# Chunk attention and two block products: another layout of the attention's score tiles, and part of one weight matrix split in place

## The chip, the cores and the metric

One Trainium2 chip, one of its cores. The metric is the device time of one execution of the kernel in microseconds, the median of several runs. The engines of the core are TensorE (PE; its weight loads are listed as PEld), VectorE (DVE), ScalarE (ACT), GpSimd (POOL) and SyncE (SP), which issues the DMA transfers.

## The reference

```python
def _attn_ref(q, k, v):                      # 8 x 8 heads x 576 x 64
    ...
    scores = scale * np.matmul(q_c, k_c.transpose(0, 1, 2, 4, 3))   # chunks of 64
    scores = scores - np.max(scores, axis=-1, keepdims=True)
    attn = np.exp(scores)
    attn = attn / (np.sum(attn, axis=-1, keepdims=True) + 1e-09)
    out = np.matmul(attn, v_c)
    ...
def reference(...):
    x = attention's output as 4608 tokens x 512
    x = square(relu(x @ moe_w_in)) @ moe_w_out        # 512 -> 2048 -> 512
    h = x @ moe2_w_in                                 # 512 -> 2048
    g = where(h >= 1, h, where(h <= -1, 0, (h + 1) ** 2 / 4))
    return g @ moe2_w_out                             # 2048 -> 512
```

All four weight matrices reach the kernel as 64-bit floats and are decoded to 32 bits on chip.

## The kernel before, in words

All large products are made in `float32r`: an operand is split into a rounded part (hi) and the rest (lo), and three products hi*hi, lo*hi, hi*lo go into one PSUM tile.

The work runs in four stages on TensorE. **Stage 1** (attention and the first matrix): the plain product `plain_h` (line 402) makes one 128x512 block `ph` of `x @ w_in` out of 12 matmuls of 512 columns, in two slots of six; there are 9 blocks of 512 tokens with 16 rows of `ph` each, so 288 slots. **Stages 2 to 4** are the three other products, done as block products with seven products P1 to P7 in place of eight (`form_b`, `form_a`, line 449 `products`).

The order of all instructions is written out by hand, with a slot number for every step: in a slot first TensorE's six matmuls are put down, then what `at_slot` has for it. Each engine does its instructions in that order.

*Attention.* A unit is four heads (two pairs `p` of two heads `e`) of two chunks `c` of 64 tokens; there are 72 units. The first 11 turns come ahead of stage 1 (`head`); after that a turn has four slots (`turn`): slot 0 has `att_d` of unit i-3, `att_b` of unit i-1 and `att_x` of unit i-3; slot 1 `att_exp` of i-1; slot 2 `att_c`, `att_ce` of i-2 and `att_n` of i-1; slot 3 `att_a`, `att_ae` of unit i. On TensorE a unit is:

- `att_a`, tile `psA` (line 291): four 128x128 transposes of q and k;
- `att_b`, tile `psB` (line 309): eight matmuls of 64x64 with 64 columns in f32, the scores. The contraction lies on the partitions of head `e`; the result goes to the partitions of chunk `c`. In the order of the loops the quadrants of the array (rows `e`, columns `c`) are (0,0), (0,1), (1,0), (1,1), and the same again for the second pair;
- `att_c`, tile `psC` (line 350): eight matmuls of 64x64 with the identity, which transpose the weights `s` of one chunk and head each; quadrants (0,0), (1,1), (0,0), (1,1) and so on;
- `att_d`, tile `psD` (line 367): eight matmuls of 64x64, the weights times v.

*Weights.* `w_out` of the first expert (m = 0) and the two matrices of the second (m = 1, 2) go through 16 units each, one every 5.1 slots from slot 22 on: `unit_a` and `unit_b` decode and round, `sums` makes three more blocks of the seven, `unit_c` casts all seven blocks (128x896) to hi on ScalarE, `unit_hi` stores hi to a DRAM tile (448 KB), `unit_d` subtracts on VectorE and stores lo (448 KB). `load_w` (line 243) later reads one product's hi and lo for both columns, 256 KB in one transfer, into one of the 56 tiles `w0` to `w55`. For m = 0 the first 24 loads (products P1, P5, P6; eight row blocks each) stand at every second slot from slot 192 on; their tiles are `w32` to `w55`, which nothing used before.

Of the kernel before, what the change touches and what calls it, by code (L numbers as in the profile page):

```python
# [8 lines left out]
F32 = mybir.dt.float32  # L9
F32R = mybir.dt.float32r  # L10
U32 = mybir.dt.uint32
AF = mybir.ActivationFunctionType
ALU = mybir.AluOpType
AX = mybir.AxisListType

P = 128

TINY = 2.0**-15 * 1.125
CH = 64
G = 32  # L20
HU = 4
NP = HU // 2
# [1 line left out]

FMAX = 3.4028234663852886e38
RANK = ("P1", "P5", "P6", "P3", "P7", "P2", "P4")
CIDX = {"P1": 0, "P2": 1, "P7": 2, "P4": 3, "P5": 4, "P6": 5, "P3": 6}
SIZES = (448, 448, 448, 480, 480)


# [1 line left out]
def chunk_attention_moe_moe2(ctx, tc, q, k, v, w_in1, w_out1, w_in2, w_out2, out):  # L32
# [10 lines left out]
    nc = tc.nc  # L43
# [4 lines left out]
    NF = DFF // P  # L48
# [4 lines left out]
    HF = NF // 2  # L53
# [5 lines left out]
    NBL = len(blocks)  # L59
# [3 lines left out]
    wp = ctx.enter_context(tc.tile_pool(name="wp", bufs=1))  # L63
# [6 lines left out]
    def f(ap):  # L70
        return ap.bitcast(F32)
# [26 lines left out]
    wd = {(m, a): dram.tile([P, 2, 2, 7, P], F32, name=f"w{m}_{a}") for m in range(3) for a in range(8)}  # L98
# [4 lines left out]


    win = {}
    wst = {}

    def bits(t, a, y):
# [71 lines left out]

    def sums(c):

        for o, x, z, op in ((4, 2, 3, ALU.add), (2, 0, 2, ALU.subtract), (5, 4, 0, ALU.subtract), (6, 1, 5, ALU.subtract)):
            nc.gpsimd.tensor_tensor(out=c[:, o], in0=c[:, x], in1=c[:, z], op=op)

    def store_parts(m, a, b, hi, lo):
        nc.sync.dma_start(out=wd[m, a][:, 0, b], in_=f(hi))
        nc.sync.dma_start(out=wd[m, a][:, 1, b], in_=f(lo))

    def unit_b(m, a, b):  # L190
        y, ab = wst[m, a, b]
        if m == 2:
            c = ep.tile([P, 4, P], F32, tag="wl", name="wq", bufs=2, padded_shape=[P, 7, P])
        else:
            c = ep.tile([P, 7, P], F32, tag="wc", name="wc", bufs=1)
        nc.vector.scalar_tensor_tensor(
            out=c[:, 0:4].rearrange("p a f -> p (a f)"), in0=ab, scalar=TINY, in1=f(y), op0=ALU.is_ge, op1=ALU.mult
        )
        wst[m, a, b] = c
        if m == 2:  # L200
            nc.sync.dma_start(out=wq[a, b], in_=c[:, 0:4])
            del wst[m, a, b]
        else:
            sums(c)

    def unit_c(*u):
        c = wst[u]
        hi = ep.tile([P, 7, P], F32R, tag="wh", name="wh", bufs=2)
        nc.scalar.copy(hi, c)
        wst[u] = (c, hi)  # L210

    def unit_hi(m, a, b):
        nc.sync.dma_start(out=wd[m, a][:, 0, b], in_=f(wst[m, a, b][1]))

    def unit_d(m, a, b):
        c, hi = wst.pop((m, a, b))
        lo = ep.tile([P, 7, P], F32R, tag="wl", name="wl", bufs=2)
        nc.vector.tensor_tensor(out=lo, in0=c, in1=f(hi), op=ALU.subtract)
        nc.sync.dma_start(out=wd[m, a][:, 1, b], in_=f(lo))


    def late_a(a, b):
# [4 lines left out]
    def late_b(a, b):  # L227
        sums(wst[a, b])
# [7 lines left out]
    def late_d(a, b):  # L236
        c, hi = wst.pop((a, b))
        nc.gpsimd.tensor_tensor(out=c, in0=c, in1=f(hi), op=ALU.subtract)
        store_parts(2, a, b, hi, c)

    wt = {}

    def load_w(m, tag, a, prod):
        t = wp.tile([P, 2, 2, P], F32R, tag=f"w{tag}", name=f"w{m}")
        nc.sync.dma_start(out=f(t), in_=wd[m, a][:, :, :, CIDX[prod]])
        wt[m, a, prod] = t
# [5 lines left out]
    def rows(par):  # L252
        return slice(par * CH, (par + 1) * CH)
# [48 lines left out]
    def att_b(u):  # L302

        qkT = att[u]
        pt = pa.tile([P, 2, 512], F32, tag="qk", name="psB")
        for p in range(NP):
            for e in range(2):
                for c in range(2):
                    nc.tensor.matmul(  # L309
                        pt[rows(c), e, p * CH:(p + 1) * CH],  # L310
                        qkT[rows(e), 0, p, rows(c)],
                        qkT[rows(e), 1, p, rows(c)],
                        start=True,
                        stop=True,
                    )
        sc = pt[:, :, 0:NP * CH].rearrange("q e (p k) -> q e p k", p=NP)
        m = ep.tile([P, 2, NP], F32, tag="m", name="m", bufs=3)
        z = ep.tile([P, NP, 2], F32, tag="z", name="z", bufs=3)
        nc.vector.tensor_reduce(out=m, in_=sc, op=ALU.max, axis=AX.X, negate=True)  # L319
        att[u] = [sc, m, z]  # L320

    def att_exp(u):
        sc, m, z = att[u]
        s = ep.tile([P, NP, 2, CH], F32, tag="s", name="s", bufs=2)
        for p in range(NP):
            for e in range(2):
                nc.scalar.activation(
                    out=s[:, p, e],
                    in_=sc[:, e, p],
                    func=AF.Exp,  # L330
                    bias=m[:, e, p:p + 1],
                    accum_out=z[:, p, e:e + 1],
                )
        att[u] = [s, z]

    def att_n(u):
        s, z = att[u]
        nc.vector.tensor_scalar_add(z, z, 1e-9)
        nc.vector.reciprocal(z, z)
        s4 = s.rearrange("q p e k -> q (p e) k")  # L340
        z4 = z.rearrange("q p e -> q (p e)")
        nc.gpsimd.tensor_tensor(out=s4, in0=s4, in1=z4.unsqueeze(2).to_broadcast([P, HU, CH]), op=ALU.mult)

    def att_c(u):
        s, _ = att[u]
        pt = pa.tile([P, NP, 2, CH], F32, tag="t", name="psC", padded_shape=[P, HU, 2, CH], bufs=2)
        for p in range(NP):
            for e in range(2):
                for c in range(2):
                    nc.tensor.matmul(  # L350
                        pt[rows(c), p, e, :], s[rows(c), p, e, :], ident[rows(c), rows(c)], start=True, stop=True
                    )
        att[u] = pt

    def att_ce(u):
        at = ep.tile([P, NP, 2, CH], F32, tag="atT", name="atT", bufs=2)
        nc.scalar.copy(at, att[u])
        att[u] = at

    def att_d(u):  # L360

        at = att[u]
        pt = pa.tile([P, 2, 512], F32, tag="d", name="psD")
        for p in range(NP):
            for c in range(2):
                for e in range(2):
                    nc.tensor.matmul(  # L367
                        pt[rows(e), c, p * CH:(p + 1) * CH],
                        vt[u // UT % NV][rows(c), u % UT * HU + 2 * p + e, :],
                        at[rows(c), p, e, :],  # L370
                        start=True,
                        stop=True,
                    )
        att[u] = pt
# [250 lines left out]
    SB1 = 2 * NF * NBL  # L625
# [19 lines left out]
    def at_slot(s, fn, *args):  # L645
        s = int(s)
        assert cur[0] is None or s >= cur[0], (s, cur)
        todo.setdefault(s, []).append((fn, args))
# [4 lines left out]
    with tc.manual_schedule():  # L653
        early = tc.tile_pool(name="early", bufs=1, side="right")
        ep = early.__enter__()
        ident = ep.tile([P, P], F32, name="ident")
        plain = tc.tile_pool(name="plain", bufs=1, space=bass.MemoryType.PSUM)
        pa = plain.__enter__()
# [89 lines left out]
        for n, u in enumerate(units):  # L748
            g = U0 + n * UPER
            if n < 2:  # L750
                at_slot(g - 3 + n, stage_unit, *u)
            at_slot(g, unit_a, *u)
            if n + 2 < len(units):
                at_slot(g, stage_unit, *units[n + 2])
            at_slot(g + 2, unit_b, *u)
            if u[0] < 2:
                at_slot(g + 4, unit_c, *u)
                at_slot(g + 5, unit_hi, *u)
                at_slot(g + 6, unit_d, *u)
# [26 lines left out]
        for w, s0 in ((0, SB1), (1, SB2)):  # L786
            for j in range(NPAIR):
                for r, prod in enumerate(RANK):
                    s = s0 + 56 * j + 8 * r
                    for kk in range(HF):  # L790
                        pe_slot(s + kk, form_b, w, j, prod, kk)
                    for kp in range(HF // 2):
                        t = s + 2 * kp - PREP
                        if j == 0 and r == 0 and w == 0:
                            t = max(t, done + 12)
# [13 lines left out]
        for j in range(NPAIR):  # L809
            for i in range(HF):  # L810
                b = SA2 + 7 * (HF * j + i)
                for prod, o in OFFS.items():
                    pe_slot(b + o, form_a, j, i, prod)
        for j in range(NPAIR):
            if j == 0:
                e = SA2
                loads = tuple(e - 24 + n for n in range(4))
                times = dict(P1=e - 14, P5=e - 11, P6=e - 8, P3=e - 6, P2=e - 3, P7=e - 2, P4=e + 1)
            else:
                b = SA2 + 7 * (HF * j - 1)  # L820
# [9 lines left out]
            if j + 1 < NPAIR:  # L830
                for n in range(4):
                    g = SA2 + 56 * j + 12 + 10 * n
                    u = divmod(4 * j + n, 2)
# [4 lines left out]
        for t in range(56):  # L838
            r, kk = divmod(t, 8)
            i, ro = divmod(t, 7)  # L840

            tag = (t + 2 * NF) % 56
            s = 2 * NF * (NBL - 3) + 2 * t if t < 24 else 2 * NF * (NBL - 1) + 2 * (t - 24) + 1 if t < 32 else SB1 + t - 30
            at_slot(s, load_w, 0, tag, kk, RANK[r])
            at_slot(SB1 + 56 * (NPAIR - 1) + t, load_w, 1, tag, i, ORD[ro])
            at_slot(SA2 + 7 * (HF * (NPAIR - 1) + i) + OFFS[ORD[ro]], load_w, 2, tag, kk, RANK[r])

# [54 lines left out]
```

## Time and profile before

| what | value |
|---|---|
| median of 3 runs | 1654.92 us (1653.35 to 1658.9) |
| the profiled execution, its own time | 1659.15 us |
| span of its trace, first to last instruction | 1657.4 us |
| TensorE busy | 1617.0 us (98%) |
| VectorE, ScalarE, GpSimd busy | 1077.6, 873.8, 422.4 us |
| DMA moved | 339.6 MB, mean 205 GB/s |

The table is read from the top of the profile: the span is what a sum of terms is made against, and the 1.75 us between span and time lie around it. An engine's busy share is a mean over four stages that differ.

### The profile page before, as it was taken

How to read it: one execution, taken by the hardware profiler on the slowest of the kernel's cores; microseconds unless marked ns; L12 is line 12 of the kernel's file. 1: busy time of each engine (PE TensorE's matmuls, PEld its weight loads, DVE VectorE, ACT ScalarE, POOL GpSimd, SP SyncE). 2: the span in 40 equal slices, each digit the busy share in tenths (PEclk: the TensorE clock that was granted, in tenths of full speed). 3: DMA queues.
4: the chain of work that ended last, by engine and by line, in shares of the span. 5: the costliest groups of instructions: out<-in, count | busy, mean ns of one | idle time of the engine just before them, and what ended most of it. 6: DMA issues, size and time to landing. Idle time of an engine off the chain costs nothing.

```text
span 1657.4 us, 29362 instructions
## 1 busy us (share of the span) xinstructions
PE 1617.0 (98%) x10512; PEld 1376.6 (83%) x10512; DVE 1077.6 (65%) x1432; ACT 873.8 (53%) x1852; POOL 422.4 (25%) x466
## 2 busy tenths in 40 slices
PE   6999999999999999999999999999999999999998
PEld 4677777777777899999888898988888899998887
DVE  6956555555444177767776757767574777877776
ACT  7656666666554244444444566756565544444442
POOL 2666666565333300000000333424330000000000
PEclk9999999999999999999999999999999999999999
DMA  9768888889996895427277765554659873554723
GB/s 211 204 202 275 275 274 271 267 271 274 268 261 217 279 275 170 132 91 224 64 224 231 214 233 191 197 199 173 226 202 342 292 200 89 146 147 100 198 41 48
DMA packets 442738, 339.60 MB, mean 205 GB/s; under 512 B 214240, under 2 KB 419040, under 8 KB 442592
## 3 DMA queue, kind: packets, MB, share of 16 engines
q1 hardware_dynamic: 442592, 337.73, 67.9%
q8 instruction: 83, 1.36, 0.3%
q14 instruction: 63, 0.52, 0.1%
HBM read 195.04 MB, written 142.61 MB: 204 GB/s over the span
## 4 chain that ended last, share of the span: by engine, by line
PE 85%; DVE 6%; DMA 3%; issue 2%; ACT 2%; POOL 1%; SPq 0%; POOLq 0%; DVEq 0%; ACTq 0%
PE X L453 31%; PE ph L411 24%; PE V L453 16%; PE W L453 7%; PE psC L350 2%; PE psA L291 2%; PE psD L367 1%; PE psB L309 1%; DVE ol L443 1%; DVE wy L118 1%; DMA w<-lc 1%; DVE t L534 1%; DVE wy L115 1%; DVE xr L447 1%; DVE wy L147 1%
## 5 line engine op out<-in xcount | busy, mean ns | idle before, releaser
L453 PE MATMUL X<-oh,w 128*128 128x448 f32 (+1 forms) x1920 | 559.1, 372 | 4.5 <-DVE c L514 4.5
L442 ACT CAST oh<-gr 128x896 fp32r<-128x896 f32 (+1 forms) x280 | 270.0, 964 | 334.9 <-PE X L453 152.1
L443 DVE TENSOR_TENSOR ol<-gr,oh 128x896 fp32r<-128x896 f32 (+1 forms) x280 | 314.3, 1124 | 182.7 <-ACT oh L442 176.9
L453 PEld LDWEIGHTS X<-oh,w 128*128 128x128 f32 x1920 | 360.7, 188 | 48.0 <-ACT t L528 4.3
L453 PE MATMUL X<-ol,w 128*128 128x448 f32 (+1 forms) x960 | 357.0, 372 | 6.8 <-POOL ol L443 5.3
L453 PE MATMUL V<-oh,w 128*128 128x448 f32 (+1 forms) x960 | 278.7, 371 | 0.0
L411 PE MATMUL ph<-xh,ih 128*128 128x512 f32 x576 | 245.9, 427 | 0.0
L411 PE MATMUL ph<-xl,ih 128*128 128x512 f32 x576 | 228.1, 396 | 0.0
L411 PE MATMUL ph<-xh,il 128*128 128x512 f32 x576 | 227.3, 395 | 0.0
L424 POOL TENSOR_TENSOR g<-g 128x512 f32<-128x512 f32 x144 | 169.1, 1174 | 187.1 <-ACT g L423 179.7
L453 PEld LDWEIGHTS X<-ol,w 128*128 128x128 f32 x960 | 180.5, 188 | 29.5 <-POOL ol L443 6.9
L453 PEld LDWEIGHTS V<-oh,w 128*128 128x128 f32 x960 | 180.2, 188 | 21.2 <-ACT s L499 0.3
L447 DVE TENSOR_TENSOR gr<-gr,gr 128x896 f32<-128x896 f32 (+1 forms) x160 | 177.7, 1111 | 2.8 <-DMA gr<-g 2.8
L453 PE MATMUL V<-ol,w 128*128 128x448 f32 (+1 forms) x480 | 177.9, 371 | 0.0
L423 ACT ACTIVATE g<-ph 128x512 f32<-128x512 f32 x144 | 86.3, 600 | 156.1 <-PE ph L411 143.3
L453 PE MATMUL W<-oh,w 128*128 128x448 f32 (+1 forms) x480 | 139.3, 371 | 0.0
L411 PEld LDWEIGHTS ph<-xh,ih 128*128 128x128 f32 x576 | 109.1, 189 | 25.5
L443 POOL TENSOR_TENSOR ol<-xr,oh 128x896 fp32r<-128x896 f32 (+1 forms) x15 | 36.6, 2442 | 364.2 <-ACT oh L442 348.8
L411 PEld LDWEIGHTS ph<-xl,ih 128*128 128x128 f32 x576 | 109.1, 189 | 24.4
L411 PEld LDWEIGHTS ph<-xh,il 128*128 128x128 f32 x576 | 109.7, 190 | 17.4
L528 ACT ACTIVATE t<-c,half 128x448 f32<-128x448 f32 (+1 forms) x120 | 81.2, 681 | 70.4 <-DVE c L514 70.4
L319 DVE TENSOR_REDUCE m<-psB 128x4 f32<-128x256 f32 x72 | 30.4, 422 | 124.6 <-PE psB L309 124.6
(69 smaller groups left out, 1980.1 us busy)
## 6 DMA issues: line engine op xcount, KB each, us to landing
w<-w SPq DMA_DIRECT2D x168, 256.0 KB, 5.0
gr<-g SPq DMA_DIRECT2D x96, 448.0 KB, 5.2
gr<-g SPq DMA_DIRECT2D x64, 480.0 KB, 4.6
g<-t SPq DMA_DIRECT2D x96, 224.0 KB, 2.6
wu<-in_moe_w_out_dram SPq DMA_DIRECT2D x64, 256.0 KB, 4.3
g<-t SPq DMA_DIRECT2D x64, 240.0 KB, 4.6
w<-wh SPq DMA_DIRECT2D x32, 448.0 KB, 3.9
w<-wl SPq DMA_DIRECT2D x32, 448.0 KB, 5.1
```

Source lines behind the costliest of these rows:

```text
L115: nc.vector.scalar_tensor_tensor(out=y, in0=w1, scalar=0xC0000000, in1=y, op0=ALU.bitwise_and, op1=ALU.bitwise_or)
L291: nc.tensor.transpose(pt[:, i, p, :], qkn[i][:, h0 + 2 * p:h0 + 2 * p + 2, :].rearrange("p h d -> p (h d)"), ident)
L319: nc.vector.tensor_reduce(out=m, in_=sc, op=ALU.max, axis=AX.X, negate=True)
L350: nc.tensor.matmul(pt[rows(c), p, e, :], s[rows(c), p, e, :], ident[rows(c), rows(c)], start=True, stop=True)
L411: nc.tensor.matmul(ph, win[fi][wi][:, kt * P:(kt + 1) * P], x[:, i, :], start=(kt == 0 and a == 0), stop=(kt == KT - 1 and a == 2),)
L423: nc.scalar.activation(out=g, in_=ph, func=AF.Relu)
L424: nc.gpsimd.tensor_tensor(out=g, in0=g, in1=g, op=ALU.mult)
L442: nc.scalar.copy(hi, raw)
L443: eng.tensor_tensor(out=lo, in0=raw, in1=f(hi), op=ALU.subtract)
L447: eng.tensor_tensor(out=o, in0=x, in1=z, op=ALU.subtract)
L453: nc.tensor.matmul(o, wt_[:, wi, c, :], x[:, i, :], start=first and a == 0, stop=last and a == 2, skip_group_check=True,)
L528: nc.scalar.activation(out=t, in_=h, func=AF.Square, bias=half, scale=0.5)
```

## The change

In the attention, the scores of a pair `p` of heads go to the partitions `p` and the chunk `c` to the free dimension (before: chunk on the partitions, pair on the free dimension). `att_b` keeps its eight matmuls and its loops, and writes to other quadrants. With this layout `att_c` takes two 128x128 transposes, one for each `e`, for its eight identity matmuls. `att_exp`, `att_n`, `att_ce`, `att_d` and the maximum keep their sizes and index the new order.

In the weights, for m = 0, the hi and lo of P1, P5 and P6 are written by `unit_c` and `unit_d` straight into the tiles `w32` to `w55`, in three casts and three subtracts of 128x128 a unit; the cast, subtract and stores that go by way of DRAM are left with four blocks of seven (128x512, 256 KB each), and the first 24 `load_w` of m = 0 fall away. `CIDX` and `sums` are numbered anew, so that these four blocks lie side by side; the number and size of the sums stay.

```diff
-CIDX = {"P1": 0, "P2": 1, "P7": 2, "P4": 3, "P5": 4, "P6": 5, "P3": 6}
+CIDX = {"P1": 0, "P2": 1, "P7": 2, "P4": 3, "P3": 4, "P5": 5, "P6": 6}
...
+    def w_tag(t):
+        return (t + 2 * NF) % 56
...
-    def unit_c(*u):
-        c = wst[u]
-        hi = ep.tile([P, 7, P], F32R, tag="wh", name="wh", bufs=2)
-        nc.scalar.copy(hi, c)
-        wst[u] = (c, hi)
+    def unit_c(m, a, b):
+        c = wst[m, a, b]
+        if m == 0:
+            for prod in RANK[:3]:
+                if b == 0:
+                    wt[0, a, prod] = wp.tile([P, 2, 2, P], F32R, tag=f"w{w_tag(RANK.index(prod) * HF + a)}", name="w0")
+                nc.scalar.copy(wt[0, a, prod][:, 0, b], c[:, CIDX[prod]])
+        r = unit_r(m)
+        hi = ep.tile([P, r.stop - r.start, P], F32R, tag="wh", name="wh", bufs=2, padded_shape=[P, 7, P])
+        nc.scalar.copy(hi, c[:, r])
+        wst[m, a, b] = (c, hi)
+
+    def unit_r(m):
+        return slice(1, 5) if m == 0 else slice(0, 7)
...
     def unit_d(m, a, b):
         c, hi = wst.pop((m, a, b))
-        lo = ep.tile([P, 7, P], F32R, tag="wl", name="wl", bufs=2)
-        nc.vector.tensor_tensor(out=lo, in0=c, in1=f(hi), op=ALU.subtract)
-        nc.sync.dma_start(out=wd[m, a][:, 1, b], in_=f(lo))
+        r = unit_r(m)
+        if m == 0:
+            for prod in RANK[:3]:
+                t = wt[0, a, prod]
+                nc.vector.tensor_tensor(out=t[:, 1, b], in0=c[:, CIDX[prod]], in1=f(t[:, 0, b]), op=ALU.subtract)
+        lo = ep.tile([P, r.stop - r.start, P], F32R, tag="wl", name="wl", bufs=2, padded_shape=[P, 7, P])
+        nc.vector.tensor_tensor(out=lo, in0=c[:, r], in1=f(hi), op=ALU.subtract)
+        nc.sync.dma_start(out=wd[m, a][:, 1, b, r], in_=f(lo))
...
             for e in range(2):
                 for c in range(2):
                     nc.tensor.matmul(
-                        pt[rows(c), e, p * CH:(p + 1) * CH],
+                        pt[rows(p), e, c * CH:(c + 1) * CH],
                         qkT[rows(e), 0, p, rows(c)],
                         qkT[rows(e), 1, p, rows(c)],
...
-        pt = pa.tile([P, NP, 2, CH], F32, tag="t", name="psC", padded_shape=[P, HU, 2, CH], bufs=2)
-        for p in range(NP):
-            for e in range(2):
-                for c in range(2):
-                    nc.tensor.matmul(
-                        pt[rows(c), p, e, :], s[rows(c), p, e, :], ident[rows(c), rows(c)], start=True, stop=True
-                    )
+        pt = pa.tile([P, 2, NP, CH], F32, tag="t", name="psC", padded_shape=[P, HU, 2, CH], bufs=2)
+        for e in range(2):
+            nc.tensor.transpose(
+                pt[:, e].rearrange("k p t -> k (p t)"), s[:, e].rearrange("q c k -> q (c k)"), ident
+            )
...
-                        at[rows(c), p, e, :],
+                        at[rows(c), e, p, :],
...
-            tag = (t + 2 * NF) % 56
-            s = 2 * NF * (NBL - 3) + 2 * t if t < 24 else 2 * NF * (NBL - 1) + 2 * (t - 24) + 1 if t < 32 else SB1 + t - 30
-            at_slot(s, load_w, 0, tag, kk, RANK[r])
+            tag = w_tag(t)
+            if t >= 24:
+                s = 2 * NF * (NBL - 1) + 2 * (t - 24) + 1 if t < 32 else SB1 + t - 30
+                at_slot(s, load_w, 0, tag, kk, RANK[r])
```

## Rows read from the trace of the kernel before

**Rows 1.** The page: TensorE over the span, granted clock in 40 slices.

```profile
PE 1617.0 (98%) x10512; PEld 1376.6 (83%) x10512; DVE 1077.6 (65%) x1432; ACT 873.8 (53%) x1852; POOL 422.4 (25%) x466
...
PEclk9999999999999999999999999999999999999999
```

**Rows 2.** Windows: PE, PEld, DVE, ACT, POOL busy (instructions); clock, DMA share, GB/s.

```profile
0.00:97.00 97.00, 75.33 (x954) 57.08 (x954) 73.71 (x130) 64.55 (x238) 47.63 (x49) 0.94 0.82 204
97.00:580.00 483.00, 482.87 (x4520) 373.82 (x4521) 237.19 (x451) 270.81 (x886) 255.37 (x317) 0.99 0.86 263
```

**Rows 3.** Waits of TensorE, whole span: in total, times, longest.

```profile
PE psB L309 <- ACT qkT L299: 8.8, 10, 2.8
PE X L453 <- POOL ol L443: 5.3, 4, 1.8
```

**Rows 4.** Timeline of TensorE, 199 to 207 us: start, us, what, records.

```profile
199.84 0.39 PE L411 MATMUL ph<-xh,ih 128*128 128x512 f32 x1
...
201.66 0.39 PE L411 MATMUL ph<-xl,ih 128*128 128x512 f32 x1
201.98 0.68 PE L350 MATMUL psC<-ident,s 64*64 64x64 f32 x16
202.59 0.50 PE L411 MATMUL ph<-xh,ih 128*128 128x512 f32 x1
202.93 0.39 PE L411 MATMUL ph<-xh,il 128*128 128x512 f32 x1
...
203.85 0.39 PE L411 MATMUL ph<-xl,ih 128*128 128x512 f32 x1
204.08 0.60 PE L291 MATMUL psA<-ident,qkn 128*128 128x128 f32 x4
...
204.75 0.40 PE L411 MATMUL ph<-xh,il 128*128 128x512 f32 x1
...
206.01 0.46 PE L367 MATMUL psD<-atT,vt 64*64 64x64 f32 x16
206.29 0.41 PE L309 MATMUL psB<-qkT 64*64 64x64 f32 x16
206.63 0.50 PE L411 MATMUL ph<-xh,ih 128*128 128x512 f32 x1
```

**Rows 5.** Windows, instructions of tile psC alone: PE, PEld, ACT, clock, DMA.

```profile
97.00:580.00 483.00, 38.83 (x912) 31.01 (x912) 21.67 (x57) 0.99 0.86 263
```

**Rows 6.** Windows, instructions of tile psB alone: PE, PEld, DVE, ACT, clock, DMA.

```profile
97.00:580.00 483.00, 23.42 (x896) 18.67 (x896) 23.79 (x56) 72.13 (x448) 0.99 0.86 263
```

**Rows 7.** The chain that ended last, up to 130 us: start, us, what.

```profile
12.02 0.70 PE psB L309 x16
12.72 1.06 PE psA L291 x4
14.51 1.01 PE psC L350 x13
...
28.22 1.00 PE psC L350 x13
...
53.91 0.71 PE psB L309 x16
```

**Rows 8.** Groups of ScalarE, then of VectorE, 97 to 580 us: busy, mean ns.

```profile
L209 ACT CAST wh<-wc 128x896 fp32r<-128x896 f32 x32 | 30.4, 951 | 1.2 <-POOL wc L184 1.2
L357 ACT COPY atT<-psC 128x256 f32<-128x256 f32 x57 | 21.7, 380 | 10.6 <-PE psC L350 10.6
...
L218 DVE TENSOR_TENSOR wl<-wc,wh 128x896 fp32r<-128x896 f32 x32 | 40.8, 1274 | 0.7 <-ACT wh L209 0.4 <-issue 0.3
L382 DVE TENSOR_TENSOR xl<-psD,xh 128x256 fp32r<-128x256 f32 x58 | 24.1, 415 | 5.1 <-ACT xh L381 5.1
```

**Rows 9.** Timeline of ScalarE, 202 to 206 us.

```profile
202.38 0.96 ACT L209 CAST wh<-wc 128x896 fp32r<-128x896 f32 x1
...
205.04 0.38 ACT L299 COPY qkT<-psA 128x256 f32<-128x256 f32 x1
```

**Rows 10.** DMA, 97 to 580 us: packets, then issues, KB each, us to landing.

```profile
DMA packets 177366, 127.16 MB, mean 263 GB/s; under 512 B 97349, under 2 KB 167063, under 8 KB 177303
...
w<-wh SPq DMA_DIRECT2D x32, 448.0 KB, 3.9
w<-wl SPq DMA_DIRECT2D x32, 448.0 KB, 5.1
...
w<-w SPq DMA_DIRECT2D x32, 256.0 KB, 4.4
```

More of the change, by code (lines that the diff above doesn't have):

```diff
@@ L105, in chunk_attention_moe_moe2 @@
     win = {}
+    wt = {}
+    def w_tag(t):
+        return (t + 2 * NF) % 56
     wst = {}
@@ L181, in sums @@
     def sums(c):
-        for o, x, z, op in ((4, 2, 3, ALU.add), (2, 0, 2, ALU.subtract), (5, 4, 0, ALU.subtract), (6, 1, 5, ALU.subtract)):
+        for o, x, z, op in ((5, 2, 3, ALU.add), (2, 0, 2, ALU.subtract), (6, 5, 0, ALU.subtract), (4, 1, 6, ALU.subtract)):
             nc.gpsimd.tensor_tensor(out=c[:, o], in0=c[:, x], in1=c[:, z], op=op)
@@ L204, in unit_b @@
             sums(c)
-    def unit_c(*u):
-        c = wst[u]
-        hi = ep.tile([P, 7, P], F32R, tag="wh", name="wh", bufs=2)
-        nc.scalar.copy(hi, c)
-        wst[u] = (c, hi)
+    def unit_c(m, a, b):
[11 more added lines that the diff above has]
+        return slice(1, 5) if m == 0 else slice(0, 7)
     def unit_hi(m, a, b):
-        nc.sync.dma_start(out=wd[m, a][:, 0, b], in_=f(wst[m, a, b][1]))
+        nc.sync.dma_start(out=wd[m, a][:, 0, b, unit_r(m)], in_=f(wst[m, a, b][1]))
     def unit_d(m, a, b):
         c, hi = wst.pop((m, a, b))
-        lo = ep.tile([P, 7, P], F32R, tag="wl", name="wl", bufs=2)
-        nc.vector.tensor_tensor(out=lo, in0=c, in1=f(hi), op=ALU.subtract)
-        nc.sync.dma_start(out=wd[m, a][:, 1, b], in_=f(lo))
+        r = unit_r(m)
[6 more added lines that the diff above has]
+        nc.sync.dma_start(out=wd[m, a][:, 1, b, r], in_=f(lo))
     def late_a(a, b):
@@ L239, in late_d @@
         store_parts(2, a, b, hi, c)
-    wt = {}
     def load_w(m, tag, a, prod):
@@ L315, in att_b @@
                     )
-        sc = pt[:, :, 0:NP * CH].rearrange("q e (p k) -> q e p k", p=NP)
-        m = ep.tile([P, 2, NP], F32, tag="m", name="m", bufs=3)
-        z = ep.tile([P, NP, 2], F32, tag="z", name="z", bufs=3)
+        sc = pt[:, :, 0:2 * CH].rearrange("q e (c k) -> q e c k", c=2)
+        m = ep.tile([P, 2, 2], F32, tag="m", name="m", bufs=3)
+        z = ep.tile([P, 2, 2], F32, tag="z", name="z", bufs=3)
         nc.vector.tensor_reduce(out=m, in_=sc, op=ALU.max, axis=AX.X, negate=True)
@@ L323, in att_exp @@
         sc, m, z = att[u]
-        s = ep.tile([P, NP, 2, CH], F32, tag="s", name="s", bufs=2)
-        for p in range(NP):
-            for e in range(2):
+        s = ep.tile([P, 2, 2, CH], F32, tag="s", name="s", bufs=2)
+        for e in range(2):
+            for c in range(2):
                 nc.scalar.activation(
-                    out=s[:, p, e],
-                    in_=sc[:, e, p],
+                    out=s[:, e, c],
+                    in_=sc[:, e, c],
                     func=AF.Exp,
-                    bias=m[:, e, p:p + 1],
-                    accum_out=z[:, p, e:e + 1],
+                    bias=m[:, e, c:c + 1],
+                    accum_out=z[:, e, c:c + 1],
                 )
@@ L339, in att_n @@
         nc.vector.reciprocal(z, z)
-        s4 = s.rearrange("q p e k -> q (p e) k")
-        z4 = z.rearrange("q p e -> q (p e)")
+        s4 = s.rearrange("q e c k -> q (e c) k")
+        z4 = z.rearrange("q e c -> q (e c)")
         nc.gpsimd.tensor_tensor(out=s4, in0=s4, in1=z4.unsqueeze(2).to_broadcast([P, HU, CH]), op=ALU.mult)
@@ L345, in att_c @@
         s, _ = att[u]
-        pt = pa.tile([P, NP, 2, CH], F32, tag="t", name="psC", padded_shape=[P, HU, 2, CH], bufs=2)
-        for p in range(NP):
-            for e in range(2):
-                for c in range(2):
-                    nc.tensor.matmul(
-                        pt[rows(c), p, e, :], s[rows(c), p, e, :], ident[rows(c), rows(c)], start=True, stop=True
-                    )
+        pt = pa.tile([P, 2, NP, CH], F32, tag="t", name="psC", padded_shape=[P, HU, 2, CH], bufs=2)
+        for e in range(2):
+            nc.tensor.transpose(
+                pt[:, e].rearrange("k p t -> k (p t)"), s[:, e].rearrange("q c k -> q (c k)"), ident
+            )
         att[u] = pt
     def att_ce(u):
-        at = ep.tile([P, NP, 2, CH], F32, tag="atT", name="atT", bufs=2)
+        at = ep.tile([P, 2, NP, CH], F32, tag="atT", name="atT", bufs=2)
         nc.scalar.copy(at, att[u])
```

## Prediction

> **What bounds the kernel now.** I read the page first: TensorE is busy 98% of the span, at full clock nearly throughout [rows 1]. A mean says nothing on where an edit pays, so next come the windows: up to 97 us TensorE works 75 of 97 us and others set the pace; from 97 to 580 us, where the attention runs between the matmuls of `ph`, it is busy 482.87 of 483 us [rows 2]. In that stage a nanosecond less on TensorE is a nanosecond less of the kernel, and one on another engine is worth nothing so long as it is not late. The waits of TensorE say the same: the longest sum is 8.8 us, `psB` waiting for the copies of q and k, in 10 waits [rows 3], of which the window leaves at most 0.13 us for the stage from 97 us on. So I price TensorE's instructions between 97 and 580 us, then look at what the other edits could make late, and last at the 97 us ahead.
>
> **The two transposes for eight matmuls.** The price of `psC` is what it adds between matmuls of `ph`. Undisturbed, eight of these take 199.84 to 201.66, 0.2275 us each. The two starting at 201.66 and 202.59 end, by the start of the next, at 202.93: 1.27 us for two where 0.455 would do, so `psC` adds 0.815 us [rows 4]. The four transposes of `psA` add in the same way (203.85 to 204.75) 0.90 - 0.455 = 0.445 us, 0.11 us each [rows 4]. Two of them for `psC`: 0.22 us, so 0.59 us less a unit. The trace has 912 records of `psC` in the stage, 16 a unit [rows 4, 5], thus 57 units: **33.6 us less**. The transposes are the same instruction at the same size as `psA`'s and stand between the same neighbours, so this term I hold for good.
>
> **The score matmuls on other quadrants.** This is the term that decides, and no row shows it. `psB` has the same eight matmuls, each of which the trace shows as two records, so 16 passes. Before, the loops visit the quadrants (0,0), (0,1), (1,0), (1,1) and again; four quadrants have four passes each, and neighbours differ. After, rows `e` and columns `p`: (0,0) twice, (1,0) twice, (0,1) twice, (1,1) twice. So four passes in a row fall on one quadrant. Rows bound what that costs:
>
> - `psD` (all four quadrants, in turn) needs 206.01 to 206.29 for 16 passes and `psB` 206.29 to 206.63, exit included; `psC`, whose 16 passes alternate between two quadrants, needs 201.98 to 202.59 for entry, passes and exit, 0.61 us, as much as `psD` and `psB` together with their 32 passes (0.62) [rows 4]. So passes run abreast: four at a time when four quadrants take turns, two at a time with two. Four at a time makes 4 steps, two at a time 8, and 4 steps more cost 0.61 - 0.34 = 0.27 us, rather too much than too little, as `psC` has an entry from 128x128 that `psB` hasn't.
> - From below: nothing, if the array takes four passes on one quadrant as easily as before, as long as rows alternate as they did (they do: four passes on rows 0, four on rows 1).
> - From above: one at a time, 16 steps, 12 more than now: 0.81 us.
>
> I take two at a time, 0.27 us: a quadrant's two matmuls stand one behind the other, as those of `psC` do on its two quadrants, and while the second runs the next quadrant may start. `psC` is the nearest row, since there too a quadrant gets more work than its turn. 896 records are 56 units [rows 6]: **15.1 us more**.
>
> TensorE's tile `psD` has the same quadrants in the same order as before, and only reads `atT` by another index: nothing.
>
> **What the layout leaves as it was.** The maximum, four exponentials, sum and reciprocal, the scaling on GpSimd and the copy `atT` have the same sizes; they cost nothing new, hidden by `ph` as now. `psC` a little earlier or `psB` a quarter of a microsecond later makes the exponentials no later than their turn, since `psC` of that unit comes a whole turn (some 7 us) later.
>
> **Weights in place: ScalarE.** For 16 units a cast of 128x896 (951 ns) becomes one of 128x512 and three of 128x128. From 951 and, for 128x256, 380 ns [rows 8], an element a partition is 0.89 ns and the start 0.15 us: about 608 + 3 x 266 = 1406 ns, 0.46 us more a unit, 7 us in all. What covers it: ScalarE is busy 271 of 483 us [rows 2]. The tightest follower I see is the copy of k: when a cast stands ahead of it in the queue, as at 202.38, it still ends at 205.42 and `psB` starts at 206.29 [rows 4, 9], 0.87 us of room, of which 0.46 would go. If the room were gone, at most these 7 us would show.
>
> **VectorE.** A subtract of 128x896 is 1274 ns, one of 128x256 415 [rows 8]: 1.34 ns an element and 72 ns start, so 758 + 3 x 244 = 1490, 0.2 us more a unit, with VectorE idle half of the stage [rows 2]. Nothing.
>
> **DMA and its queue.** Sixteen units store 2 x 192 KB less, and 24 loads of 256 KB are gone: 6.1 and 6.1 MB, of 127 MB that move in the stage [rows 10], a tenth. Every transfer that fell away was issued by SP ahead of its need and TensorE waited for none [rows 3]; so nothing comes back as time. It is a cover, though: should the stage become shorter, DMA, at a share of 0.86 [rows 2], has less to do in it. The tiles `w32` to `w55` have no earlier user, so the new writes wait for nobody. From 580 us on TensorE starts stage 2 with these tiles made long before.
>
> **Ahead of 97 us.** Here the chain alternates between VectorE's decoding and the attention. `psB` stands on it with 0.7 us or a little less a time, about 7 times (the first and the sixth are shown), `psC` twice with 1.0 us [rows 7]. `psB` with 4 more steps costs there 0.27 us, up to twice that where the clock is at its lower level (`psA` takes 1.06 there [rows 7], against some 0.45 us in the stage): 7 x 0.4 = 2.8 us more. `psC` by two transposes at half of `psA`'s 1.06 is 0.5 us less, twice: 1.0 less. Sum: **1.8 us more**.
>
> **Sum.** -33.6 + 15.1 + 1.8 = -16.7 us. Against the profiled execution's own 1659.15 us that is 1642.4; this execution lies 4.2 us above the median of its runs, so I forecast 1654.9 - 16.7 = **1638 us**.
>
> **Rivals.**
>
> *Quadrants cost nothing.* For it: only the column half of the quadrant changes; the rows alternate as before. Against it: `psC` shows that passes need different quadrants to run abreast. Time: -33.6, and -1 ahead of 97 us: 1620 us. Chance 0.2.
>
> *The weights of the second matmul on a quadrant can't be loaded while the first one's passes run.* The row beside it: in `psC` and in `psD` every change of matmul is also one of rows within at most four passes, and both run with loads hidden [rows 4], so a repeated quadrant isn't in the trace. As a mechanism: of each four passes two run, then a step goes by with the loads of the next two, and then these run: 3 steps for each four, 12 where there were 4, so 8 more, 0.54 us x 56 = 30.2 us, and some 5.6 us in place of 2.8 ahead of 97 us: -33.6 + 30.2 + 4.6 = +1 us, 1656 us. Chance 0.22. The Trainium skill has this rule (TensorE: Matmul & The Clock Gate, Part 3: Packing small matmuls, the mechanism): weight loads run beside matmuls in flight only where the row groups differ. By that rule the change would be worth about nothing; that every load in the rows of `psC`, `psD` and `psB` is hidden agrees with it, but none of them tests it.
>
> *One pass at a time (the other side).* The place is `psB`; four passes on a quadrant run one after the other, and the next quadrant, later in the queue, starts only when they are done. 12 steps more: 0.81 x 56 = 45.4 us, and some 8 us ahead of 97 us: -33.6 + 45.4 + 7 = +19 us, 1674 us. It turns the sign once `psB` takes over 0.59 us more. For it: TensorE takes its instructions in order; the four transposes of `psA`, all on one tile, come one by one at 0.11 us. Against it: `psC`'s two passes of a matmul on one quadrant run at the rate of two abreast. Chance 0.18.
>
> *The gain is made and lost to a later wait*, ScalarE's 7 us above or the DMA queue: it would take 7 us off the forecast, 1645 us; the room of 0.87 us speaks against it. It is within the likeliest one's range, 1632 to 1645.
>
> **How the numbers follow.** The forecast case has the other 0.4. About 0.3% (5 us) is what a measurement here can tell from no change. Faster: 0.4 + 0.2 and a quarter of the load rival, 0.65; within: most of that rival, 0.15; slower: the one-by-one case and the rest, 0.20. The range reaches from the first rival, 1620, to the load rival with 5 us on top, and leaves out the one-by-one case: 1619 to 1662.
>
> **What the profile after would show.** `psC` with two records of 128x128 a unit that add 0.22 us between matmuls of `ph`; `psB` from its start to the next `ph` 0.61 us (0.34 if the first rival holds, 0.88 for the load rival, 1.15 one by one); the stage from 97 us on still 100% TensorE and about 18 us shorter, the next stages as long as before; 24 transfers `w<-w` fewer, and no new wait of TensorE. The forecast is wrong if `psB` is not near 0.61, or if TensorE shows waits for `qkT` or `s` in the stage.

## The result and the profile after

The changed kernel takes **1628.8 us** (median of 4 runs, 1626.96 to 1630.68) against 1655.2 us (4 runs): ratio 0.9838, 95% interval 0.9817 to 0.9859, so 26.4 us less. The forecast was 1638 us in a range of 1619 to 1662. The profiled execution has a span of 1628.9 us, 28.5 less than that of before.

The page, its lines of all engines; it answers to [rows 1]:

```profile
PE 1587.7 (97%) x9504; PEld 1364.4 (84%) x9504; DVE 1095.0 (67%) x1480; ACT 873.4 (54%) x1900; POOL 428.0 (26%) x466
```

TensorE lost 29.3 us of work, about what the kernel lost in time. ScalarE's busy time stayed, VectorE's rose by 17 us, and neither shows in the time. Where TensorE's work went is in its timeline between the matmuls of `ph` (start, us, what, records), the answer to [rows 4]:

```profile
198.79 0.60 PE L310 MATMUL psA<-ident,qkn 128*128 128x128 f32 x4
...
200.38 0.40 PE L428 MATMUL ph<-xl,ih 128*128 128x512 f32 x1
200.71 0.46 PE L384 MATMUL psD<-atT,vt 64*64 64x64 f32 x16
200.99 0.47 PE L328 MATMUL psB<-qkT 64*64 64x64 f32 x16
201.40 0.50 PE L428 MATMUL ph<-xh,ih 128*128 128x512 f32 x1
...
204.02 0.39 PE L428 MATMUL ph<-xl,ih 128*128 128x512 f32 x1
204.25 0.38 PE L367 MATMUL psC<-ident,s 128*128 128x128 f32 x2
204.39 0.48 PE L428 MATMUL ph<-xh,ih 128*128 128x512 f32 x1
204.70 0.40 PE L428 MATMUL ph<-xh,il 128*128 128x512 f32 x1
```

Read as before: the two matmuls of `ph` around `psC` take 204.02 to 204.70, 0.68 us where 0.455 would do, so `psC` now adds 0.225 us; before it added 0.815. `psB` needs 200.99 to 201.40, 0.41 us from its start to the next `ph`; before 0.34 [rows 4]. In the single records of the trace, which the timeline merges, the median of all units in the stage is 0.404 us, before 0.344: **0.06 us more**. The forecast had 0.61, 0.27 more.

The windows, all engines, clock, DMA share, GB/s; they answer to [rows 2], but the second one now reaches 28 us into the next stage, so the third shows the attention's stage alone:

```profile
0.00:97.00 97.00, 77.62 (x744) 57.85 (x744) 72.20 (x127) 62.52 (x233) 48.38 (x48) 0.96 0.80 200
97.00:580.00 483.00, 480.07 (x3858) 385.65 (x3859) 276.58 (x520) 285.52 (x954) 259.72 (x318) 1.00 0.85 255
...
98.75:551.80 453.05, 451.87 (x3720) 359.77 (x3721) 254.55 (x498) 270.07 (x933) 258.05 (x317) 1.00 0.83 252
```

From 97 us on TensorE has an idle of 2.9 us where it had 0.13: 1.75 us are the end of one wait at 98.75 us, and 1.2 lie behind it (453.05 less 451.87). Its waits over the whole span (total, times, longest), beside [rows 3]:

```profile
PE psB L328 <- ACT qkT L318: 11.5, 13, 4.9
PE X L470 <- POOL ol L460: 6.2, 4, 1.8
```

The timeline of TensorE has the place of the longest, and the start of the next stage; first the kernel before, then the changed one:

```profile
97.13 0.70 PE L309 MATMUL psB<-qkT 64*64 64x64 f32 x16 [2.79 <-ACT qkT L299]
...
579.77 0.57 PE L453 MATMUL X<-oh,w 128*128 128x448 f32 x2
```

```profile
98.75 0.62 PE L328 MATMUL psB<-qkT 64*64 64x64 f32 x16 [4.88 <-ACT qkT L318]
...
551.80 0.57 PE L470 MATMUL X<-oh,w 128*128 128x448 f32 x2
```

It is the same `psB`, the 17th. Up to this `psB` the changed kernel is 1.6 us late, and from there to the next stage it needs 551.80 - 98.75 = 453.05 us for 482.64: **29.6 us less**. From 57 units' `psC` and 56 units' `psB`, 57 x 0.59 - 56 x 0.06 = 33.6 - 3.4 = 30.2 should come, less the 1.2 us that TensorE now stands idle there: 29.0, within 0.6 of what was measured. The stages behind take another 0.5 us less, together 28.5.

### The profile page after: what moved, and what is told of

It is laid out like the page before. It is cut to its first block, busy times and chain, and to the rows that moved or that the text cites. A ratio compares the mean times of both kernels' runs of the same rounds, so it can differ in the third digit from the quotient of the medians.

```text
span 1628.9 us, 27413 instructions
## 1 busy us (share of the span) xinstructions
PE 1587.7 (97%) x9504; PEld 1364.4 (84%) x9504; DVE 1095.0 (67%) x1480; ACT 873.4 (54%) x1900; POOL 428.0 (26%) x466
## 4 chain that ended last, share of the span: by engine, by line
PE 87%; DVE 5%; DMA 2%; ACT 2%; issue 2%; POOL 1%; SPq 0%; POOLq 0%; ACTq 0%; DVEq 0%
PE X L470 34%; PE ph L428 22%; PE V L470 17%; PE W L470 8%; PE psA L310 1%; PE psD L384 1%; PE psB L328 1%; POOL ol L460 1%; PE psC L367 1%; DMA wu<-in_moe_w_out_dram 1%; ACT s L346 1%; DMA ws<-in_moe_w_in_dram 1%; DVE ol L460 1%; DVE wy L121 1%; DVE wy L124 1%
## 5 line engine op out<-in xcount | busy, mean ns | idle before, releaser
L551 DVE SCALAR_TENSOR_TENSOR t<-c,t 128x448 f32<-128x448 f32 (+1 forms) x120 | 95.5, 822 | 18.2 <-ACT t L545 18.0
```

The costliest lines, as they stand in the source:

```text
L551: nc.vector.scalar_tensor_tensor(out=t, in0=h, scalar=1.0, in1=t, op0=ALU.max, op1=ALU.min)
```

## The experiments

Three theories were set against each other on why a `psB` with four passes in a row on one quadrant costs little. A is the prediction's: quadrants run side by side, and passes on one quadrant one after the other. B: what costs is a change of rows, and passes on the same rows go together whatever their columns. C: `psC` was slow because both its rows write into one bank (one section) of PSUM.

**Rows outermost in the old `psC`** (kernel before; eight passes on quadrant (0,0), then eight on (1,1)).

```diff
-        for p in range(NP):
-            for e in range(2):
-                for c in range(2):
+        for c in range(2):
+            for p in range(NP):
+                for e in range(2):
                     nc.tensor.matmul(
                         pt[rows(c), p, e, :], s[rows(c), p, e, :], ident[rows(c), rows(c)], start=True, stop=True
```

> The kernel before, with the eight identity matmuls of psC ordered by rows: all of quadrant (0,0), then all of (1,1); nothing else. Theory A (quadrants run abreast, the step of the prediction): one quadrant at a time, 16 steps for 8, psC from its start to the next ph 0.61 -> about 1.1 us, kernel about 1683 us. Theory B (what costs is a change of rows; passes on the same rows go together whatever the columns): 2 changes of rows for 8, psC 0.61 -> about 0.25 us, 0.35 x 57 = 20 us less, about 1635 us. Theory C (psC is slow because both rows write into one PSUM bank): about as before, 0.61 us, 1655 us.

Measured: 1670.4 us, ratio to the kernel before 1.0091 (1.0073 to 1.0108). Its timeline of TensorE:

```profile
202.96 0.96 PE L350 MATMUL psC<-ident,s 64*64 64x64 f32 x16
203.85 0.50 PE L411 MATMUL ph<-xh,ih 128*128 128x512 f32 x1
```

`psC` takes 0.89 us in place of 0.61. B and C fall: B wanted a drop, C no change. A has the right side, but not the size: 16 steps one by one would be 1.1 us. The two quadrants still overlap, though eight passes on the first stand ahead of the second.

**Rows outermost in the new `psB`** (changed kernel).

```diff
-        for p in range(NP):
-            for e in range(2):
+        for e in range(2):
+            for p in range(NP):
                 for c in range(2):
                     nc.tensor.matmul(
                         pt[rows(p), e, c * CH:(c + 1) * CH],
```

> The changed kernel, with the loop over e (the rows) outermost in att_b, so psB does eight passes on rows 0 and then eight on rows 1; a quadrant's four passes still stand together. Theory A: no fewer steps, 0.41 us or more, 1629 us or slower. Theory B: two runs of rows in place of four, psB 0.41 -> about 0.29 us, 0.12 x 56 = 7 us less, about 1622 us. Theory C: 0.41 us as it is, 1629 us (the two rows write to two banks in either order).

Measured: 1630.1 us, 0.9843 (0.9824 to 0.9861); the changed kernel's own ratio is 0.9838. `psB` from its start to the next `ph`:

```profile
206.93 0.47 PE L328 MATMUL psB<-qkT 64*64 64x64 f32 x16
207.34 0.50 PE L428 MATMUL ph<-xh,ih 128*128 128x512 f32 x1
```

0.41 us, as with rows in the middle loop. Against B; with A (and C, which the run before had already refuted, wanted the same).

**Rows innermost in the new `psB`** (changed kernel, loops p, c, e: two passes on a quadrant, then the other rows).

```diff
         for p in range(NP):
-            for e in range(2):
-                for c in range(2):
+            for c in range(2):
+                for e in range(2):
                     nc.tensor.matmul(
                         pt[rows(p), e, c * CH:(c + 1) * CH],
```

> The changed kernel, with the loop over e (the rows) innermost in att_b: rows change at every matmul, neighbours lie on quadrants with different rows. Theory A: neighbours on two quadrants, two abreast, and no four on one quadrant: 0.41 us or less, 1629 us or faster. Theory B: 8 runs of rows in place of 4, 4 steps of about 0.06 us more, psB 0.41 -> about 0.65 us, 0.24 x 56 = 13 us more, about 1642 us. Theory C: 0.41 us or less, 1629 us.

Measured: 1626.8 us, 0.9829 (0.9809 to 0.9849). `psB` from its start to the next `ph`:

```profile
207.21 0.47 PE L328 MATMUL psB<-qkT 64*64 64x64 f32 x16
207.61 0.50 PE L428 MATMUL ph<-xh,ih 128*128 128x512 f32 x1
```

0.40 us. B wanted 0.65 and is done with. That the rows change between two matmuls of `psB` or not makes no difference of more than 0.01 us. Nor is it four in a row as such that costs: here no quadrant has more than two passes in a row, but the program gives two quadrants all their passes before the other two get their first, and the time is nearly the same.

**The attention alone** (changed kernel, weights of m = 0 as before).

```diff
-        if m == 0:
-            for prod in RANK[:3]:
...
-        return slice(1, 5) if m == 0 else slice(0, 7)
...
-            if t >= 24:
+            s = 2 * NF * (NBL - 3) + 2 * t if t < 24 else 2 * NF * (NBL - 1) + 2 * (t - 24) + 1 if t < 32 else SB1 + t - 30
+            at_slot(s, load_w, 0, tag, kk, RANK[r])
```

> The changed kernel with the weights of m = 0 as in the kernel before (all seven parts by way of DRAM, all 56 loads): the attention's part of the change alone. If the weights in place are worth nothing, as predicted: 1629 us, within 2 us. Rival, that the tenth of the DMA traffic that they save is worth time: 1632 us or more. Rival, that their longer casts cost: 1626 us or less.

Measured: 1626.4 us, 0.9827 (0.9810 to 0.9844), beside 0.9838 (0.9817 to 0.9859) for the whole change: the intervals overlap almost wholly. The median is 2.4 us under the changed kernel's, outside the 2 us that were expected and near the rival's 1626, so the median alone doesn't rule out that the longer casts cost something; two further runs below take that up. The trace rules it out to 0.4 us: from the 17th `psB` to the next stage this run needs 551.52 - 98.86 = 452.66 us, for 453.05 with the weights in place. The attention carries all of the gain.

After these four runs the theory was sharpened to D: each quadrant takes its passes alone and in order, and TensorE hands passes on to a quadrant some three ahead of the one that runs, so that four in a row on one quadrant still let the others start, and eight don't. The single records of `psC` in the trace, two at a time, stand 0.058 us apart.

**Fours on a quadrant in the old `psC`** (kernel before, loops p, c, e).

```diff
         for p in range(NP):
-            for e in range(2):
-                for c in range(2):
+            for c in range(2):
+                for e in range(2):
                     nc.tensor.matmul(
                         pt[rows(c), p, e, :], s[rows(c), p, e, :], ident[rows(c), rows(c)], start=True, stop=True
```

> The kernel before, with the loops of psC as p, c, e: four passes on quadrant (0,0), four on (1,1), and again. Theory D (each quadrant takes a pass in about 0.058 us, alone and in order; TensorE hands passes on to a quadrant some three ahead of the one that runs, so four in a row on one quadrant keep the next ones fed, eight don't): psC 0.61 to 0.67 us as before, kernel 1655 to 1659 us. Theory B2 (what costs is the number of passes in a row on a quadrant, from two on, in proportion): halfway between 0.61 for two in a row and 0.89 for eight, about 0.70 us, 0.09 x 57 = 5 us more, 1661 us.

Measured: 1657.1 us, 1.0009 (1.0000 to 1.0019). Its timeline of TensorE:

```profile
207.91 0.73 PE L350 MATMUL psC<-ident,s 64*64 64x64 f32 x16
208.57 0.50 PE L411 MATMUL ph<-xh,ih 128*128 128x512 f32 x1
```

0.66 us: the 0.05 over 0.61 is within D's bounds, and B2's 5 us lie outside the interval, which ends at 3.1 us. So two, four and eight in a row give 0.61, 0.66 and 0.89 us: no straight line, but a bend somewhere between four and eight.

The single records of the two traces show where it lies (which quadrant a record belongs to follows from its place in the program; the units of the stage agree to 2 ns). With eight in a row, the first quadrant's passes start 0, 0.107, 0.165, 0.223 and 0.282 us after the first, and the second quadrant's first weight load follows at 0.287: when the fifth pass has started and three more wait. With four in a row it comes at 0.013 us: when the first pass has started and three wait. So what D calls "some three" is three in both.

**Quadrants in turn** (changed kernel, loops c, e, p in `att_b`, so that the order of the quadrants is that of the kernel before).

```diff
-        for p in range(NP):
+        for c in range(2):
             for e in range(2):
-                for c in range(2):
+                for p in range(NP):
                     nc.tensor.matmul(
                         pt[rows(p), e, c * CH:(c + 1) * CH],
```

> The changed kernel with the loops of att_b as c, e, p, so that the quadrants follow one another as in the kernel before: (0,0), (0,1), (1,0), (1,1), and again; each quadrant still has four passes. Theory D: the 0.06 us that psB took longer is the late start of three of the four quadrants, so psB is 0.34 us from its start to the next ph again, 0.06 x 56 = 3.5 us less, about 1625 us. Rival, that the other halves of PSUM or of the array cost the 0.06: 0.40 us as in the changed kernel, 1629 us.

Measured: **1625.1 us**, 0.9823 (0.9805 to 0.9840); with the next run, the fastest that was made. Its timeline of TensorE:

```profile
207.66 0.41 PE L328 MATMUL psB<-qkT 64*64 64x64 f32 x16
208.01 0.50 PE L428 MATMUL ph<-xh,ih 128*128 128x512 f32 x1
...
548.94 0.57 PE L470 MATMUL X<-oh,w 128*128 128x448 f32 x2
```

`psB` is back at 0.35 us (the median of the units is 0.343, before 0.344), and the next stage starts at 548.94 in place of 551.80, 2.9 us sooner (3.5 were expected). The medians differ by 3.7 us, the ratios, each to the kernel before in its own series, by 2.5 us; the intervals overlap, so this rests on the timeline more than on the medians. The rival, that the other halves of array or PSUM cost something, falls: the quadrants are the same ones, only their order differs.

**The same with the attention alone** (weights of m = 0 as before, as in the run above).

> As the run with the quadrants in turn, with the weights of m = 0 as in the kernel before. If the weights in place are worth nothing: the same as that run within 2 us, about 1625 us. If they cost the 2 us by which the attention alone came out below the changed kernel: about 1623 us.

Measured: 1624.8 us, 0.9810 (0.9794 to 0.9825), 0.3 us from the run with the weights in place. From the 17th `psB` to the next stage the two need 449.92 and 450.18 us. This pair too gives the weights nothing.

**The weights alone** (kernel before, with the whole second half of the change and none of the first).

> The kernel before with the weights of m = 0 made in place and nothing else: the other half of the change. Predicted: nothing, 1655 us within 2 us, with TensorE as full as before from 97 us on. Rival, that it costs by the longer casts: 1657 us or more, with waits for qkT. Rival, that it saves DMA time that shows: 1653 us or less.

Measured: 1656.1 us, 1.0004 (0.9992 to 1.0015). The window from 97 us on:

```profile
97.00:580.00 483.00, 482.91 (x4520) 374.14 (x4521) 251.22 (x499) 274.27 (x935) 247.82 (x317) 0.99 0.78 237
```

The DMA packets of the same stretch:

```profile
DMA packets 164732, 114.64 MB, mean 237 GB/s; under 512 B 96968, under 2 KB 154429, under 8 KB 164669
```

12.5 MB less move, the DMA share falls from 0.86 to 0.78 [rows 2, 10], VectorE has 14 us and ScalarE 3 us more, and TensorE is as full as it was, to 0.04 us.

**The weight units two slots later** (the run with the quadrants in turn, `U0` from 22 to 24).

```diff
-    U0, UPER = 22, 5.1
+    U0, UPER = 24, 5.1
```

> As the run with the quadrants in turn (1625.1 us), with the 48 weight units beginning at slot 24 in place of 22. There TensorE waits 4.65 us at 98.8 us for the copies of q and k, which stand on ScalarE behind the decode of the first unit, whose data lands late; before the change the same wait was 2.8 us, so about 2 us of the attention's gain ahead of 97 us go into it. If that is so: two slots later (some 3.5 us) most of that wait is gone, the stage ends about 3 us sooner, 1622 us. Rival, that VectorE's decoding of the pieces sets the pace there anyway: the wait moves to another instruction, 1625 us. Rival, that the last units now come too late for the next stage: a new wait at its start, over 1625 us.

Measured: 1625.5 us, 0.9814 (0.9794 to 0.9834): nothing gained. TensorE's wait is gone from 98.8 us and stands 14 us further on. Its timeline there:

```profile
112.61 0.70 PE L384 MATMUL psD<-atT,vt 64*64 64x64 f32 x16 [4.70 <-ACT atT L374]
```

The timeline of ScalarE just before:

```profile
111.62 0.69 ACT L117 ACTIVATE wa<-wu 128x512 f32<-128x512 f32 x1 [6.26 <-DMA wu<-in_moe_w_out_dram]
```

And the timeline of the DMA issues (SP) ahead of that:

```profile
99.85 5.00 SPq L447 DMA_DIRECT2D g<-g  x4
104.94 0.40 SPq L295 DMA_DIRECT2D qkn<-in_q_dram  x1
105.43 0.53 SPq L295 DMA_DIRECT2D qkn<-in_k_dram  x1
106.07 1.42 SPq L174 DMA_DIRECT2D wu<-in_moe_w_out_dram  x2
```

The decode of a unit waits for its load `wu`, which is issued at 106.07, behind stores of `g` that hold the queue for 5 us while they wait for `g`. The first rival's outcome, a wait that moves, came; the cause that it gave, VectorE's decoding, isn't what the rows show. What would shorten the wait, another place of the loads in the queue, wasn't tried.

## Why the prediction was right, and which term was mis-sized

The direction and the range came out, and the term that carries them, the transposes, came out as worked out. The middle did not: 1628.8 us lies 9 us under the 1638, and outside the 1632 to 1645 that the prediction gave its likeliest case. That the number still lies inside is owed to a wide range, which left out one case alone. By the prediction's own signs it was wrong on `psB`, which is not near 0.61 us, and on TensorE's waits: 1.2 us of them are new in the stage.

*What bounds the kernel.* Right: the gain was made in the stage from 97 us on, on TensorE, 29.6 us there; 1.6 are lost ahead of it and 0.5 won behind, 28.5 in all.

*Two transposes for eight matmuls.* Right in size: 0.815 to 0.225 us a unit, 0.59 less as worked out, since the same instruction stood in the trace between the same neighbours.

*The score matmuls on other quadrants.* This is the term that was mis-sized: "I take two at a time, 0.27 us". It measured 0.06 (0.404 for 0.344), 3.4 us in the stage and not 15.1, which is the forecast's miss in the stage: 29.6 us measured, 18.5 forecast. What was right is that quadrants run side by side and a quadrant takes its passes one by one: the run with eight in a row costs 0.28 us, the others 0.06 at most. What was wrong is to take the rate of `psC` as what a repeated quadrant costs. `psC` had two quadrants for 16 passes, so eight on each; `psB` has four on each in either order, and TensorE reaches far enough ahead to feed all four. What is left, 0.06, falls away when the quadrants take turns. It is a delay at the start: in the single records the weight loads for the first passes on the other three quadrants come 0.06 to 0.09 us after that for the first, where before all four came within 0.02 us, under the end of `psD`. The lower bound, nothing, was much nearer than the row that I took to be nearest.

*The load rival* (three steps for each four) is refuted by 0.41 against its 0.88, and *one pass at a time* by 0.41 against 1.15. The rule that the Trainium skill has on this (TensorE: Matmul & The Clock Gate, Part 3: Packing small matmuls, the mechanism), that weight loads run beside matmuls only where the row groups differ, would have left the loads of each four's second pair in the open; with all eight passes of the same rows in a row (the run with the rows outermost) `psB` stayed at 0.41 us. The prediction's remark that the hidden loads of `psC`, `psD` and `psB` agree with the rule was a misreading: a matmul's two passes have the same rows, and in the single records of the old `psC` the load for a quadrant's next pass comes 0.004 us after the pass before it has started. No row here bears the rule out for 64x64 tiles; the measurement decides.

*Weights in place.* Right: nothing, 1.0004 (0.9992 to 1.0015) alone. The costs were there and were hidden: by busy time the three casts and the fourth take 22.1 us for 16 units, 1.38 each (1.41 forecast), the four subtracts 28.3 us, 1.77 each (1.49 forecast, since a subtract of 128x128 took 416 ns on the mean and not 244). From the groups of ScalarE, then of VectorE, 97 to 552 us of the changed kernel, beside [rows 8]:

```profile
L219 ACT CAST w<-wc 128x128 fp32r<-128x128 f32 x48 | 12.0, 317 | 3.3 <-POOL wc L190 3.2
L222 ACT CAST wh<-wc 128x512 fp32r<-128x512 f32 x16 | 10.1, 629 | 1.7 <-POOL wc L190 1.4
...
L237 DVE TENSOR_TENSOR w<-wc,w 128x128 fp32r<-128x128 f32 x48 | 17.4, 416 | 0.0
L239 DVE TENSOR_TENSOR wl<-wc,wh 128x512 fp32r<-128x512 f32 x16 | 10.9, 680 | 0.0
```

*Ahead of 97 us.* The forecast was 1.8 us more, and 1.6 was measured at the 17th `psB`, but that is luck, not the reason given. TensorE is ready for it at 98.75 - 4.88 = 93.87 us, 0.5 us sooner than before (94.34), so there the attention costs nothing more; it then waits 2.1 us longer, behind a weight load that lands late. With the quadrants in turn (`psB` at 0.35 us) the same `psB` starts at the same time (98.76), so its length isn't what makes the delay. The delay's size changes from run to run: with the rows outermost or innermost, `psB` as long, it starts at 98.15 and 97.97 us. (The term was also read unevenly: `psA`'s 1.06 us run from its first start to its last end, which in the stage is 0.60 and not 0.45 [rows 4].) The timeline of the DMA issues, before and then after:

```profile
88.60 0.42 SPq L276 DMA_DIRECT2D qkn<-in_q_dram  x1
89.11 0.53 SPq L276 DMA_DIRECT2D qkn<-in_k_dram  x1
89.74 1.28 SPq L168 DMA_DIRECT2D wu<-in_moe_w_out_dram  x2
```

```profile
88.82 2.06 SPq L295 DMA_DIRECT2D qkn<-in_q_dram  x1
90.97 0.53 SPq L295 DMA_DIRECT2D qkn<-in_k_dram  x1
91.61 1.14 SPq L174 DMA_DIRECT2D wu<-in_moe_w_out_dram  x2
```

The weight load `wu` is issued 1.9 us later, and 1.6 of that stand in the issue of the load of q ahead of it, not in the stores of `g`, which end at nearly the same time (88.51 and 88.74); in the last run it is they that hold `wu` back. What held the load of q isn't shown.

## What to carry to other kernels

When small matmuls share the array, count the passes on each quadrant and look at the order: with four quadrants taking turns, 16 passes of 64x64 in f32 cost 0.34 us, with two quadrants ahead of the other two, or four passes in a row on each, 0.40, and with two quadrants 0.61 or, eight in a row, 0.89. A price from a tile that has twice the work on each quadrant isn't the price of another order of the same work; ask what the row differs in before taking it as the nearest. Eight matmuls with the identity that only transpose (0.815 us between other matmuls) are dear beside two whole transposes (0.225 us), and a layout that allows these is worth more than traffic removed from a DMA queue that TensorE doesn't wait for.

## What the runs showed of the hardware that was not expected

Passes on different quadrants overlap even when the program puts four of one quadrant ahead of the next quadrant's first (0.40 us for 16 passes, 0.34 in turn), and in part with eight ahead (0.89 us, where one after the other would be some 1.1). The single records give the reach: in the runs with four and with eight in a row, and in the changed kernel's `psB`, the next quadrant's first weight load comes within 0.013 us of the moment from which no more than three passes of the quadrant before still wait behind one that has started.
